# z^T for both row halves by transposes of shifted block pairs, attention matmuls in program order, and the first z turned between score groups

## Chip, cores, metric

The kernel runs on one core of one Trainium2 chip. The metric is the device time of one execution in microseconds (us), the median of several runs. All runs quoted here were fast, that is, none took over 1.5% longer than the fastest run of the same kernel.

## The reference

Shortened:

```python
def _attn_ref(u, v, z):                     # u, v: (8, 3008, 256), z: (8, 3008, 64)
    scores = (1.0 / S) * np.matmul(z, z.transpose(0, 2, 1))
    attn = np.maximum(scores, 0.0) ** 2
    return u * np.matmul(attn, v)
# x is that result as (24064, 256); w_in: (256, 2048), w_out: (2048, 256)
h = x @ w_in
return (h * np.cos(h)) @ w_out
```

The scores are symmetric, so only the 21 block groups on and above the diagonal are computed for each of the 8 batches; the others come from a transpose by DMA (`tt`).

## The kernel before

Four kinds of matmul share TensorE: **S** (scores, contraction over 64 rows), **A** (attention times v), **H** (x times w_in) and **Y** (times w_out). S contracts only 64 rows, so two S matmuls can run at once, one in the upper and one in the lower half of the array. For that, z^T must lie in both halves of the partitions. The kernel before gets it by copying each block of z beside itself on VectorE (DVE) and letting a DMA transpose turn the pair:

```python
    def load_z(b, g):                       # three times per batch, for the batch to come
        n, full, rest = rows(z, b, g)
        j0 = g * G
        nc.gpsimd.dma_start(zst[:, j0:j0 + n, 0, :], full)      # fp32 to fp16, from DRAM
        ...
        nc.vector.tensor_copy(zst[:, j0:j0 + G, 1, :], zst[:, j0:j0 + G, 0, :])
        nc.sync.dma_start_transpose(zT[b % 2][:, j0:j0 + G, :], ...)

    def s_group(b, c, R):
        ...
        t = apool.tile([P, K, K, P], FP16, name="a")            # 8 buffers
        sps = [ps_w.tile([P, CW], FP32, name="w") for k in range(K)]
        for k in reversed(range(K)):
            h = slice((k % 2) * dqk, (k % 2 + 1) * dqk)         # which half of the array
            mm = nc.tensor.matmul(sps[k], zt[h, R * K + k, :], zcols[h, :], start=True, stop=True)
            if k < K - 1:
                tc.keep_in_program_order(mm)
        ...   # ACT: rt = relu(sps); DVE: a = rt * rt
        if R > c:                                               # the mirrored block
            nc.sync.dma_start_transpose(tt..., t...)

    # one chunk of 512 rows: 48 A matmuls into the one acc, then on DVE
    #     x = acc * ut              (ut: u transposed by DMA)
    # H: c16 = cos on ACT, then on DVE g = hp * c16; Y consumes g
```

A scheduler fixes each engine's order when the program is built; on the chip each engine runs its own list in that order. The first z is turned by TensorE in a phase of its own (DVE doubles it, 24 transposes, copies back) before anything else. "Head" below means the first 100 us.

## Time and profile before

| | before |
|---|---|
| median time, us (lowest to highest, 3 runs) | 1407.57 (1403.28 to 1409.5) |
| span of the profiled run, us | 1404.0 |
| TensorE busy | 95% |
| third x starts on DVE (third chunk of attention done), us | 110.2 |
| DVE idle until a z load landed, us | 98.3 |

From the page of the kernel before: the span, TensorE's busy time, the granted TensorE clock in 40 slices of the span (tenths, 9 is 90% or more), and the chain of waits by line. In the profile PE is TensorE, PEld its loading of weights, DVE VectorE, ACT ScalarE, POOL GpSimd and SP SyncE, which issues the DMA transposes; L206 is line 206 of the kernel, x7512 a count, and `out<-in` names what is written and read.

```profile
span 1404.0 us, 19607 instructions
...
PE 1330.1 (95%) x7512; PEld 682.3 (49%) x7512; DVE 782.9 (56%) x1213; ACT 878.8 (63%) x1520; POOL 105.7 (8%) x132
...
PEclk9979999999999999999999999999999999999999
...
PE acc L206 31%; PE w L237 22%; PE yp L256 21%; DMA zst<-in_z_dram 6%; PE w L163 5%; DVE g L244 2%; DMA ut<-ust 2%; ACT rt L170 2%; DMA zT_63<-zst 1%; DVE a L173 1%; SPq L178 1%; DMA zf_82<-in_z_dram 0%; DMA zT_62<-zst 0%; POOL zst L82 0%; POOL ust L103 0%
```

A busy share of 95% looks like a kernel with nothing to win but the last 5%. The chain of waits says otherwise: 6% of the span on it is the load of z, which TensorE does not use for another batch.

Waits of DVE (what it waited for, us in total, times, longest):

```profile
DVE a L173 <- ACT rt L170: 235.3, 289, 7.3
DVE zst L85 <- DMA zst<-in_z_dram: 98.3, 18, 14.2
```

The second line is 98.3 us in 18 waits of DVE for the z load. The copy at L85 itself takes 0.29 us. But DVE runs its list in order, so everything behind the copy waits with it. The Trainium skill ("TensorE: Matmul & The Clock Gate", Part 1, on queue depths) calls the ACT and DVE queues strict FIFO; this trace agrees, for example at 491 us. First DVE, then TensorE, in the timeline (start, duration; in brackets the idle time before and who ended it):

```profile
490.88 0.69 DVE L244 TENSOR_TENSOR g<-w,c_4600 128x512 f16<-128x512 f32 x1 [1.53 <-ACT c_4600 L241]
496.08 0.29 DVE L85 COPY zst<-zst 128x512 f16<-128x512 f16 x1 [4.51 <-DMA zst<-in_z_dram]
496.29 0.68 DVE L244 TENSOR_TENSOR g<-w,c_4611 128x512 f16<-128x512 f32 x1
```

```profile
492.16 0.60 PE L163 MATMUL w<-zT_63 64*128 64x512 f16 x4
492.70 0.61 PE L256 MATMUL yp<-w_out_71,g 128*128 128x256 f16 x4
497.02 1.01 PE L237 MATMUL w<-x,w_in_70 128*128 128x512 f16 x2 [3.72 <-DVE g L244]
497.83 1.06 PE L256 MATMUL yp<-w_out_71,g 128*128 128x256 f16 x4
```

DVE stood 4.5 us until the z load landed; the multiplication that makes g came right behind the copy; TensorE stood 3.7 us for that g. And the matmuls after the stop run at half speed: two H matmuls take 1.01 us where they took 0.59 elsewhere. Waits of TensorE from 100 us on, and three stretches of 175 us (start:end, length, busy time and instructions of PE, PEld, DVE, ACT, POOL, then granted clock, DMA share, GB/s):

```profile
PE w L237 <- DVE g L244: 20.3, 29, 4.0
PE w L163 <- DVE g L244: 13.3, 9, 3.7
```

```profile
350.00:525.00 175.00, 166.12 (x941) 85.16 (x940) 98.78 (x155) 110.45 (x192) 12.34 (x15) 0.98 0.54 89
525.00:700.00 175.00, 164.96 (x952) 86.35 (x950) 99.20 (x155) 111.41 (x193) 13.22 (x16) 0.98 0.63 98
700.00:875.00 175.00, 164.37 (x938) 85.61 (x936) 97.33 (x151) 109.61 (x189) 13.23 (x16) 0.97 0.58 96
```

TensorE waited 33.6 us for g, and the granted clock of 0.98, 0.98 and 0.97 is 3.5 + 3.5 + 5.25 = 12 us of full clock not granted. In the head, the timeline of TensorE has S and A alternating one by one:

```profile
15.89 0.60 PE L163 MATMUL w<-zT_62 64*128 64x512 f16 x1
16.43 0.61 PE L206 MATMUL acc<-a,v_0_64 128*128 128x512 f16 x1
16.98 0.60 PE L163 MATMUL w<-zT_62 64*128 64x512 f16 x1
```

Steps of 0.54 us each, where a warm A matmul takes 0.216. The head is also where the DVE stalls are longest. The ends of the first three chunks on DVE:

```profile
58.37 1.22 DVE L223 TENSOR_TENSOR x<-acc,ut 128x1024 f16<-128x1024 f32 x1
...
88.48 1.22 DVE L223 TENSOR_TENSOR x<-acc,ut 128x1024 f16<-128x1024 f32 x1
...
110.23 1.22 DVE L223 TENSOR_TENSOR x<-acc,ut 128x1024 f16<-128x1024 f32 x1
```

To see how much of the head is lost I priced every matmul with the warm steps of the timeline (0.2165 us for 512 columns, 0.108 for 256, 0.53 for an unbroken group of four S): the whole program is about 1230 us of work by that price, and the first 100 us hold about 36 us of it. This is an estimate worked out from the trace.

### The profile page before, as it was taken

What the parts mean: (1) busy time and instruction counts of PE and PEld (TensorE: products, weight loads), DVE (VectorE), ACT (ScalarE), POOL (GpSimd) and SP (SyncE); (2) the same over time, 40 slices, a digit from 0 to 9 for tenths busy, and PEclk for the clock granted to TensorE, in tenths of its full rate; (3) what the DMA queues carried; (4) which work ended last, traced back from release to release, by engine and by line L of the source; (5) the groups of instructions that cost most, each with busy time, mean ns of one, the idle gap of its engine ahead of it and who ended that gap; (6) DMA issues with size and microseconds to landing.
All of it is one profiled execution on the core that took longest, in us unless ns stands there. A gap on an engine that the chain in (4) does not pass through costs nothing.

```text
span 1404.0 us, 19607 instructions
## 1 busy us (share of the span) xinstructions
PE 1330.1 (95%) x7512; PEld 682.3 (49%) x7512; DVE 782.9 (56%) x1213; ACT 878.8 (63%) x1520; POOL 105.7 (8%) x132
## 2 busy tenths in 40 slices
PE   7769999999999989999898998999999999999998
PEld 1224555445545445454454544555555555555555
DVE  3227564655655555565564655566556556565644
ACT  3337675766666656666565665666666767666645
POOL 3210010000100101000010000100001000000000
PEclk9979999999999999999999999999999999999999
DMA  9994586745836449565494544946559525543201
GB/s 186 179 145 79 88 111 109 124 77 94 119 75 101 84 72 138 86 105 86 75 139 79 103 82 70 146 90 103 91 99 133 98 61 88 102 82 83 61 23 46
DMA packets 447998, 137.13 MB, mean 98 GB/s; under 512 B 397472, under 2 KB 447648, under 8 KB 447904
## 3 DMA queue, kind: packets, MB, share of 16 engines
q1 hardware_dynamic: 323728, 81.53, 32.9%
q0 software_dynamic: 97568, 29.44, 21.3%
q10 hardware_dynamic: 26608, 24.91, 5.9%
q8 instruction: 58, 0.95, 0.3%
q14 instruction: 36, 0.29, 0.1%
HBM read 59.64 MB, written 24.64 MB: 60 GB/s over the span
## 4 chain that ended last, share of the span: by engine, by line
PE 79%; DMA 9%; ACT 4%; DVE 3%; issue 2%; POOL 1%; SPq 1%; POOLq 0%; DVEq 0%; ACTq 0%
PE acc L206 31%; PE w L237 22%; PE yp L256 21%; DMA zst<-in_z_dram 6%; PE w L163 5%; DVE g L244 2%; DMA ut<-ust 2%; ACT rt L170 2%; DMA zT_63<-zst 1%; DVE a L173 1%; SPq L178 1%; DMA zf_82<-in_z_dram 0%; DMA zT_62<-zst 0%; POOL zst L82 0%; POOL ust L103 0%
## 5 line engine op out<-in xcount | busy, mean ns | idle before, releaser
L170 ACT ACTIVATE rt<-w 128x512 f16<-128x512 f32 x672 | 350.6, 601 | 190.2 <-PE w L163 154.8
L237 PE MATMUL w<-x,w_in_70 128*128 128x512 f16 x1504 | 435.8, 382 | 24.7 <-DVE g L244 20.3
L256 PE MATMUL yp<-w_out_71,g 128*128 128x256 f16 x3008 | 450.7, 274 | 1.7 <-ACT ob L264 1.4
L256 PEld LDWEIGHTS <-g 128*128 128x128 f16 x3008 | 287.5, 98 | 220.6 <-issue 62.3
L173 DVE TENSOR_TENSOR a<-rt 128x1024 f16<-128x1024 f16 x336 | 231.1, 691 | 235.3 <-ACT rt L170 235.3
L237 PEld LDWEIGHTS <-w_in_70 128*128 128x128 f16 x1504 | 144.7, 98 | 107.2 <-issue 58.2
L206 PE MATMUL acc<-a,v_2_66 128*128 128x512 f16 x352 | 93.6, 386 | 6.7 <-DVE a L173 6.7
L163 PE MATMUL w<-zT_62 64*128 64x512 f16 x336 | 77.7, 408 | 19.2 <-ACT rt L170 11.1
L264 ACT ACTIVATE ob<-yp 128x512 f32<-128x512 f32 x94 | 56.3, 599 | 58.2 <-PE yp L256 58.2
L206 PE MATMUL acc<-a,v_2_69 128*128 128x512 f16 x352 | 90.4, 379 | 0.0
L103 POOL DMA_DIRECT2D ust<-in_u_dram x48 | 44.4, 928 | 565.7 <-DMA ut<-ust 520.7
L206 PE MATMUL acc<-tt,v_0_64 128*128 128x512 f16 (+1 forms) x288 | 75.0, 387 | 0.0
L206 PE MATMUL acc<-tt,v_0_67 128*128 128x512 f16 (+1 forms) x288 | 71.9, 376 | 0.0
L206 PE MATMUL acc<-a,v_1_65 128*128 128x512 f16 x224 | 65.6, 412 | 4.0 <-DVE x L223 3.9
L223 DVE TENSOR_TENSOR x<-acc,ut 128x128 f16<-128x128 f32 (+7 forms) x89 | 60.3, 715 | 14.0 <-PE acc L206 14.0
L163 PE MATMUL w<-zT_63 64*128 64x512 f16 x336 | 60.8, 382 | 6.2 <-DVE g L244 6.2
L206 PEld LDWEIGHTS <-v_1_65 128*128 128x128 f16 x384 | 37.7, 100 | 59.3 <-issue 24.1
L85 DVE COPY zst<-zst 128x512 f16<-128x512 f16 x21 | 6.2, 294 | 103.5 <-DMA zst<-in_z_dram 98.3
L206 PEld LDWEIGHTS <-v_0_64 128*128 128x128 f16 x384 | 37.9, 100 | 51.8 <-issue 16.2
L206 PEld LDWEIGHTS <-v_2_66 128*128 128x128 f16 x384 | 37.0, 99 | 51.6 <-issue 15.1
L206 PE MATMUL acc<-a,v_1_68 128*128 128x512 f16 x224 | 59.2, 380 | 0.0
L206 PEld LDWEIGHTS <-v_0_67 128*128 128x128 f16 x384 | 37.2, 98 | 42.5 <-issue 4.0
(1547 smaller groups left out, 1368.4 us busy)
## 6 DMA issues: line engine op xcount, KB each, us to landing
out_dram<-ob ACTq DMA_DIRECT2D x94, 256.0 KB, 3.5
ust<-in_u_dram POOLq DMA_DIRECT2D x32, 256.0 KB, 5.9
ust<-in_u_dram POOLq DMA_DIRECT2D x16, 224.0 KB, 6.1
v_0_64<-in_v_dram POOLq DMA_DIRECT2D x4, 512.0 KB, 6.1
v_1_65<-in_v_dram POOLq DMA_DIRECT2D x4, 512.0 KB, 7.1
v_0_67<-in_v_dram POOLq DMA_DIRECT2D x4, 512.0 KB, 6.1
v_1_68<-in_v_dram POOLq DMA_DIRECT2D x4, 512.0 KB, 6.4
tt<-a SPq DMA_TRANSPOSE x120, 5.0
```

Source lines behind the costliest of these rows:

```text
L85: nc.vector.tensor_copy(zst[:, j0:j0 + G, 1, :], zst[:, j0:j0 + G, 0, :])
L103: nc.gpsimd.dma_start(ust[:, dh, 0:n, :], full[:, :, ds])
L163: mm = nc.tensor.matmul(sps[k], zt[h, R * K + k, :], zcols[h, :], start=True, stop=True)
L170: nc.scalar.activation(rt[:, i, :], sps[k0 + i], AF.Relu)
L173: nc.vector.tensor_tensor(tv, rv, rv, ALU.mult)
L178: nc.sync.dma_start_transpose(tt.rearrange("p s k w -> p (s k) w"), t.rearrange("p s k w -> p (s k w)"))
L206: nc.tensor.matmul(acc[:, nh, 0:wn], vt[:, j % G, nh * P:(nh + 1) * P], a, start=(n == 0), stop=(n == NJ - 1))
L223: nc.vector.tensor_tensor(xs[m][:, :, at:at + n], acc[:, :, o:o + n], ut[:, :, i0:i0 + n], ALU.mult)
L237: nc.tensor.matmul(hp, w_in16[:, k, ft * P:(ft + 1) * P], x[:, k, :], start=(k == 0), stop=(k == NDH - 1))
L244: nc.vector.tensor_tensor(gs[(m, ft // FG)][:, ft % FG, :], hp, c16, ALU.mult)
L256: nc.tensor.matmul(ys[m][:, ts % YP, :], gs[(m, ft // FG)][:, ft % FG, ts * P:(ts + 1) * P], w_out16[:, ft, :], start=(n % (YP * NFT) == 0 ...
L264: nc.scalar.activation(ob, ys[m], AF.Copy, bias=0.0, scale=inv_s2)
```

## The change

The intent: no DVE copy. Blocks of z are stored with a zero block at each end, and the transposes take pairs of neighbouring blocks: pair k holds block k-1 and block k, so after the transpose the upper half of the partitions holds one block and the lower half the next, and every block appears in both halves at neighbouring places. Besides, S and A matmuls are tied to program order, the first z is turned between score groups, the first chunk's attention starts earlier, and some preparation moves to other engines.

```diff
-    zst = kpool.tile([P, NJ, 2, dqk], FP16, name="zst")
+    zst = kpool.tile([P, NJ + 2, dqk], FP16, name="zst")
-        nc.vector.tensor_copy(zst[:, j0:j0 + G, 1, :], zst[:, j0:j0 + G, 0, :])
-        nc.sync.dma_start_transpose(
-            zT[b % 2][:, j0:j0 + G, :],
-            zst[:, j0:j0 + G].rearrange("p j h d -> p (j h d)"))
+        for k in range(2):                  # after all three loads of the batch
+            n = (NJ + 2) // 2 - k
+            nc.sync.dma_start_transpose(
+                zT[b % 2][:, k:k + 2 * n - 1:2, :],
+                zst[:, k:k + 2 * n, :].rearrange("p j d -> p (j d)"))
 ... (s_group)
-            mm = nc.tensor.matmul(
-                sps[k], zt[h, R * K + k, :], zcols[h, :], start=True, stop=True)
-            if k < K - 1:
-                tc.keep_in_program_order(mm)
+            lo = k % 2
+            j0 = c * K + 1 - lo
+            chain(nc.tensor.matmul(         # chain: an edge to the S or A matmul before it
+                sps[k], zt[h, R * K + k + 1 - lo, :],
+                zt[h, j0:j0 + K, :].rearrange("p j w -> p (j w)"), start=True, stop=True))
 ... (attention)
-                    nc.tensor.matmul(acc[:, nh, 0:wn], ...)
+                    chain(nc.tensor.matmul(acc[:, nh, 0:wn], ...))
 ... (schedule)
+            early = 10 if b == c == 0 else 0
-                at(b * span + c * U + q, 2, qs[q])
+                at(b * span + c * U + q - early * (1 - q / U), 2, qs[q])
-            for g in range(NG):
-                at(t + (1.0 + 0.75 * g) * U, 0, lambda b=b, g=g: load_z(b, g))
+            at(t + 1.5 * U, 0, lambda b=b: load_z(b))
 ... (cut: the first phase in its own pools goes; first_z_load and first_z_turn become
      scheduled events; ust and v memsets go to POOL; a dummy Relu loads ACT's table early)
```

More of the change, by code (lines that the diff above doesn't have):

```diff
@@ L58 @@
     nc.vector.memset(pihalf, float(math.pi / 2.0))
-    zst = kpool.tile([P, NJ, 2, dqk], FP16, name="zst")
+    zst = kpool.tile([P, NJ + 2, dqk], FP16, name="zst")
     ust = kpool.tile([P, NDH, G, P], FP16, name="ust")
-    zT = [kpool.tile([P, NJ, P], FP16, name=f"zT{i}") for i in range(2)]
+    zT = [kpool.tile([P, NJ + 1, P], FP16, name=f"zT{i}") for i in range(2)]
     vs = [[kpool.tile([P, G, D], FP16, name=f"v{i}_{g}") for g in range(NG)]
           for i in range(2)]
+    ident = kpool.tile([P, P], FP16, name="ident")
     w_in16 = kpool.tile([P, NDH, Dff], FP16, name="w_in16")
     w_out16 = kpool.tile([P, NFT, D], FP16, name="w_out16")
-    for i in range(2):
-        nc.vector.memset(vs[i][NG - 1][:, G - 1, :], 0.0)
     def rows(src, b, g):
@@ L77, in rows, with load_z @@
         return n, full, rest
-    def load_z(b, g):
-        n, full, rest = rows(z, b, g)
-        j0 = g * G
-        nc.gpsimd.dma_start(zst[:, j0:j0 + n, 0, :], full)
-        if rest is not None:
-            nc.gpsimd.dma_start(zst[0:JLAST, j0 + n, 0, :], rest)
-        nc.vector.tensor_copy(zst[:, j0:j0 + G, 1, :], zst[:, j0:j0 + G, 0, :])
-        nc.sync.dma_start_transpose(
-            zT[b % 2][:, j0:j0 + G, :],
-            zst[:, j0:j0 + G].rearrange("p j h d -> p (j h d)"))
+    def load_z(b):
+        for g in range(NG):
+            n, full, rest = rows(z, b, g)
+            j0 = g * G + 1
+            nc.gpsimd.dma_start(zst[:, j0:j0 + n, :], full)
+            if rest is not None:
+                nc.gpsimd.dma_start(zst[0:JLAST, j0 + n, :], rest)
+        for k in range(2):
[3 more added lines that the diff above has]
+                zst[:, k:k + 2 * n, :].rearrange("p j d -> p (j d)"))
     def load_v(b, g):
@@ L110, in load_u @@
         uts[(b, g)] = ut
-    with tc.tile_pool(name="first", bufs=1) as fpool, \
-            tc.tile_pool(name="ps_first", bufs=NG, space=bass.MemoryType.PSUM) as fps:
-        zf = [fpool.tile([P, G, dqk], FP32, name=f"zf{g}") for g in range(NG)]
-        ident = fpool.tile([P, P], FP16, name="ident")
-        make_identity(nc, ident)
-        nc.vector.memset(zf[NG - 1][:, G - 1, :], 0.0)
-        for g in range(NG):
-            n, full, rest = rows(z, 0, g)
-            eng = (nc.sync, nc.scalar, nc.sync)[g % 3]
-            eng.dma_start(zf[g][:, 0:n, :], full)
-            if rest is not None:
-                eng.dma_start(zf[g][0:JLAST, n, :], rest)
-        for g in range(NG):
-            load_v(0, g)
-        for g in range(NG):
-            j0 = g * G
-            for h in range(2):
-                nc.vector.tensor_copy(zst[:, j0:j0 + G, h, :], zf[g])
-            tp = fps.tile([P, G, P], FP16, name="tp")
-            for j in range(G):
-                nc.tensor.transpose(
-                    tp[:, j, :], zst[:, j0 + j].rearrange("p h d -> p (h d)"), ident)
-            nc.vector.tensor_copy(zT[0][:, j0:j0 + G, :], tp)
-        nc.vector.memset(zst[:, NJ - 1, 0, :], 0.0)
     psum = lambda name, bufs: ctx.enter_context(
@@ L150, with first_z_load, first_z_turn, chain @@
     ps_y = psum("ps_y", 1)
+    zfs = {}
+    def first_z_load(g):
+        zfs[g] = xpool.tile([P, NDH, TW], FP16, name="x")
+        zf = zfs[g].rearrange("p h w -> p (h w)").bitcast(FP32).rearrange(
+            "p (j d) -> p j d", d=dqk)
+        zfs[g] = zf
+        n, full, rest = rows(z, 0, g)
+        eng = (nc.sync, nc.scalar, nc.sync)[g % 3]
+        if rest is not None:
+            nc.vector.memset(zf[:, n, :], 0.0)
+        eng.dma_start(zf[:, 0:n, :], full)
+        if rest is not None:
+            eng.dma_start(zf[0:JLAST, n, :], rest)
+    def first_z_turn(g):
+        j0 = g * G
+        last = g == NG - 1
+        nc.vector.tensor_copy(zst[:, j0 + 1:j0 + 1 + G, :], zfs[g])
+        for k, n in ((0, G), (G, 1))[0:1 + last]:
+            tp = ps_w.tile([P, CW], FP32, name="w").bitcast(FP16).rearrange(
+                "p (j w) -> p j w", w=P)
+            for i in range(n):
+                nc.tensor.transpose(
+                    tp[:, i, :],
+                    zst[:, j0 + k + i:j0 + k + i + 2, :].rearrange("p j d -> p (j d)"),
+                    ident)
+            nc.vector.tensor_copy(zT[0][:, j0 + k:j0 + k + n, :], tp[:, 0:n, :])
     fresh = {}
     turned = {}
+    before = []
+    def chain(mm):
+        if before:
+            tc.add_manual_dep(
+                mm.ins, before.pop().name,
+                mybir.DependencyInfo(
+                    mybir.DependencyClass.NoSync, mybir.DependencyReason.DATA),
+                reason="order")
+        before.append(mm.ins)
     def s_group(b, c, R):
         zt = zT[b % 2]
-        zcols = zt.rearrange("p j w -> p (j w)")[:, c * CW:(c + 1) * CW]
         t = apool.tile([P, K, K, P], FP16, name="a")
@@ L161, in s_group @@
         for k in reversed(range(K)):
-            h = slice((k % 2) * dqk, (k % 2 + 1) * dqk)
-            mm = nc.tensor.matmul(
-                sps[k], zt[h, R * K + k, :], zcols[h, :], start=True, stop=True)
-            if k < K - 1:
-                tc.keep_in_program_order(mm)
+            lo = k % 2
+            h = slice(lo * dqk, (lo + 1) * dqk)
+            j0 = c * K + 1 - lo
+            chain(nc.tensor.matmul(
+                sps[k], zt[h, R * K + k + 1 - lo, :],
+                zt[h, j0:j0 + K, :].rearrange("p j w -> p (j w)"),
+                start=True, stop=True))
         for k0 in range(0, K, 2):
@@ L205, in quantum @@
                 for nh in range(NDH):
-                    nc.tensor.matmul(
+                    chain(nc.tensor.matmul(
                         acc[:, nh, 0:wn], vt[:, j % G, nh * P:(nh + 1) * P], a,
-                        start=(n == 0), stop=(n == NJ - 1))
+                        start=(n == 0), stop=(n == NJ - 1)))
             if (q + 1) * per >= NJ:
@@ L295 @@
         if b == 0:
-            base = -100.0
-            at(base, 0, lambda: load_u(0, 0))
-            at(base + 1, 0, lambda: nc.gpsimd.dma_start(
+            for g in range(NG):
+                at(-100 + g, 0, lambda g=g: first_z_load(g))
+                at(-30 + 4.5 * g if g == 0 else -14.5 + 4.57 * (g - 0.5), 0,
+                   lambda g=g: first_z_turn(g))
+                at(-80 + g, 0, lambda g=g: load_v(0, g))
+            at(-70, 0, lambda: load_u(0, 0))
+            at(-69, 0, lambda: nc.gpsimd.dma_start(
                 w_in16, moe_w_in.rearrange("(k p) f -> p k f", p=P)))
-            at(base + 2, 0, lambda: nc.gpsimd.dma_start(
+            at(-68, 0, lambda: nc.gpsimd.dma_start(
                 w_out16, moe_w_out.rearrange("(k p) f -> p k f", p=P)))
-            at(base + 3, 0, lambda: load_u(0, 1))
+            at(-67, 0, lambda: load_u(0, 1))
         else:
             t = (b - 1) * span
-            for g in range(NG):
-                at(t + (1.0 + 0.75 * g) * U, 0, lambda b=b, g=g: load_z(b, g))
+            at(t + 1.5 * U, 0, lambda b=b: load_z(b))
             for g in range(NG):
@@ L313, with prepare @@
         at(t + 3.0 * U, 0, lambda b=b: load_u(b, 2))
-    nc.vector.memset(ust, 0.0)
+    dummy = kpool.tile([P, 1], FP32, name="dummy")
+    def prepare():
+        nc.scalar.activation(dummy, pihalf, AF.Relu)
+        make_identity(nc, ident)
+        nc.vector.memset(zst[:, 0, :], 0.0)
+        nc.vector.memset(zst[:, NJ + 1, :], 0.0)
+        nc.gpsimd.memset(ust, 0.0)
+        for i in range(2):
+            nc.gpsimd.memset(vs[i][NG - 1][:, G - 1, :], 0.0)
+    at(-90, 0, prepare)
     events.sort(key=lambda e: e[:3])
```

## The prediction

> **What bounds the kernel now.** TensorE: the page shows PE busy 95% of 1404 us; in the stage table 1050 to 1225 us is busy 173.8 of 175. In the timeline a warm 512-column matmul starts every 0.2165 us, a 256-column one every 0.108, and an unbroken score group (four K=64 matmuls, two in each half of the array) takes 0.53. At these prices the 7512 matmuls are about 1235 us of work (estimate). Laid on the timeline, the first 100 us hold only 36 us of work, 100 to 850 loses about 80 us, and 850 to the end 1.65 us per 50.
>
> **What the change removes.**
> 1. The 21 DVE copies of z (294 ns each) are cheap, but DVE runs in order: the waits view charges 98 us of DVE idle to them, for the z load (5.8 us to landing). The chain of waits gives these loads 5.6%. 35 us lie in the head (two of 14.2 and 13.3). From 122 to 848 us there are 14 stalls of 2 to 7 us; PE idles behind the late g for about 30 us there, and the granted clock falls to 0.97 in places, which I price at 8 to 10 us. The shifted transposes move 25 blocks per batch instead of 24: no new cost.
> 2. Order. From 15 to 49 us score and attention matmuls alternate one by one, 0.54 us each. The Trainium skill, "TensorEngine Tiling (Array Packing)", Key Properties, says that changing the tiling mode drains the engine; the trace agrees (warm, alternating ones step 0.31 us, not 0.2165). The new head is S4 A6 S4 A6. But h and y matmuls can still split score groups: single score matmuls fall only from 84 runs to 56, the gain nearly all in the head. A split group costs about 1.1 us more, so 15 to 20 us of splits stay.
> 3. Start: first score at about 7 us instead of 11.5, the ACT table load (1.28 us) hidden, c=0 attention earlier.
>
> **What it adds.** Memsets on POOL ahead of the v loads, delaying v, u and weights by an estimated 3 us.
>
> **The head after.** ACT paces it: 4 activations in 2.06 us per group against 0.53+1.30 us of PE. The first x still needs the u transpose, which landed at 30.7 us (now about 33), and the third chunk needs a turned block queued on SP behind the second u transpose (issued at 41.65) and two transposes of about 5 us: about 60 us. I put the third x at 65 us instead of 110.2: 45 us won.
>
> **Sum.** 45 (head) + 38 (stalls and cold clock after 100 us) = 83: span about 1321, measured about 1325 us, 80% range 1306 to 1346. Faster by over 2%: 0.96; same 0.035; slower 0.005.
>
> **What would show each step.** No DVE waits on z loads; PE waits on g in 400 to 850 us falling from about 27 us to under 6; PEclk 1.0 in all slices after the first three; third x at 60 to 70 us; first 100 us holding about 75 us of work; score matmul busy time falling by 15 to 25 us of 138; split groups between 100 and 550 us still there; last 550 us unchanged.
>
> **What would make it wrong.** Head: the DMA queues (mean share over 1.0 in the first 80 us) may hold turned blocks or u back longer, so that it wins only 30; or PE stays at the slow clock while ACT paces it, since the skill ("TensorE: Matmul & The Clock Gate", Part 1) makes the clock follow recent activity, and before stayed slow to about 50 us. Middle: SP waits for all of z and delays turned blocks. Or split groups vanish: down to 1305.

## The result

| | before | after |
|---|---|---|
| median time, us (lowest to highest, 4 runs) | 1407.67 (1403.28 to 1409.5) | 1333.43 (1332.07 to 1333.52) |
| span of the profiled run, us | 1404.0 | 1331.7 |
| third x starts on DVE, us | 110.2 | 81.1 |
| priced work in the first 100 us (estimate as above) | about 36 | about 62 |
| S matmul busy time, us | 138.5 | 122.1 |

The ratio after to before is 0.9475 (95% interval 0.9452 to 0.9497), so 5% faster. Ratios here are the mean time of one kernel's fast runs over that of the other's of the same rounds, so not quite the ratio of the medians.

The page of the changed kernel, the same parts:

```profile
span 1331.7 us, 19537 instructions
...
PE 1293.3 (97%) x7513; PEld 675.3 (51%) x7513; DVE 777.1 (58%) x1188; ACT 876.8 (66%) x1521; POOL 107.9 (8%) x135
...
PEclk9899999999999999999999999999999999999999
...
PE acc L224 36%; PE w L255 25%; PE yp L274 24%; PE w L181 6%; ACT rt L188 2%; DVE g L262 2%; DMA tt<-a 1%; DMA ut<-ust 1%; DMA x<-in_z_dram 0%; DVE a L191 0%; DVE x L241 0%; ACT ob L282 0%; ACT L259 0%; DVE zT_62 L155 0%; SPq L139 0%
```

The z load of the later batches is gone from the chain; the one left is the first batch's. DVE's waits:

```profile
DVE a L191 <- ACT rt L188: 255.0, 310, 4.4
...
DVE a L191 <- DMA tt<-a: 10.2, 1, 10.2
DVE x L241 <- DMA ut<-ust: 5.2, 1, 5.2
DVE zst L146 <- DMA x<-in_z_dram: 4.4, 2, 3.8
```

What is left on DVE for z (L146) is the first batch's cast. Two new entries, 10.2 and 5.2 us, are waits for DMA transposes, and both lie in the head. TensorE's waits for g from 100 us on and the three stretches:

```profile
PE w L255 <- DVE g L262: 4.8, 22, 0.3
```

```profile
350.00:525.00 175.00, 173.51 (x1012) 90.75 (x1011) 103.74 (x159) 117.60 (x205) 13.26 (x16) 1.00 0.62 101
525.00:700.00 175.00, 173.61 (x1026) 91.88 (x1025) 106.80 (x164) 118.61 (x206) 13.26 (x16) 1.00 0.64 105
700.00:875.00 175.00, 173.80 (x1028) 92.16 (x1025) 105.45 (x162) 120.47 (x209) 13.25 (x16) 1.00 0.60 100
```

The wait for g fell from 33.6 to 4.8 us and the clock is 1.00. In the head, TensorE and DVE:

```profile
11.07 2.09 PE L224 MATMUL acc<-a,v_0_64 128*128 128x512 f16 x6
...
13.63 1.47 PE L224 MATMUL acc<-a,v_0_64 128*128 128x512 f16 x6
...
35.78 2.72 PE L224 MATMUL acc<-a,v_0_64 128*128 128x512 f16 x6 [6.33 <-DVE x L241]
...
64.67 1.01 PE L224 MATMUL acc<-a,v_2_66 128*128 128x512 f16 x2 [5.84 <-DVE a L191]
```

```profile
34.51 1.23 DVE L241 TENSOR_TENSOR x<-acc,ut 128x1024 f16<-128x1024 f32 x1 [5.24 <-DMA ut<-ust]
...
63.93 1.29 DVE L191 TENSOR_TENSOR a<-rt 128x1024 f16<-128x1024 f16 x2 [10.23 <-DMA tt<-a]
...
81.06 1.21 DVE L241 TENSOR_TENSOR x<-acc,ut 128x1024 f16<-128x1024 f32 x1
```

A comes in runs of six and S in groups of four now, warm (six A in 1.47 us) from 13.6 us on. But then TensorE stands: at 35.8 us behind the first x, and at 64.7 us behind an `a` tile. After each stop the clock is slow again (six A in 2.72 us), as the Trainium skill ("TensorE: Matmul & The Clock Gate", Part 1) has it for a TensorE that has stood idle for some microseconds. The chain of waits shows what both waited for:

```profile
22.67 11.74 DMA ut<-ust
...
51.25 12.55 DMA tt<-a
```

A transpose of u took 11.7 us and one of a score tile 12.6 us from issue to release. Over this whole run a u transpose lands in a median of 4.8 us and a score tile's in 4.7.

Of the 72.3 us of span, 29.2 were won by the end of the third chunk (110.2 to 81.1) and 43.1 after it (1293.8 to 1250.6 us from there to the end).

### The profile page after: what moved, and what is told of

Read it like the earlier page. It is cut to its first block, busy times and chain, and to the rows that moved or that the text cites. A ratio compares the mean times of both kernels' runs of the same rounds, so it can differ in the third digit from the quotient of the medians.

```text
span 1331.7 us, 19537 instructions
## 1 busy us (share of the span) xinstructions
PE 1293.3 (97%) x7513; PEld 675.3 (51%) x7513; DVE 777.1 (58%) x1188; ACT 876.8 (66%) x1521; POOL 107.9 (8%) x135
## 4 chain that ended last, share of the span: by engine, by line
PE 90%; ACT 4%; DVE 2%; DMA 2%; issue 1%; SPq 0%; DVEq 0%; ACTq 0%
PE acc L224 36%; PE w L255 25%; PE yp L274 24%; PE w L181 6%; ACT rt L188 2%; DVE g L262 2%; DMA tt<-a 1%; DMA ut<-ust 1%; DMA x<-in_z_dram 0%; DVE a L191 0%; DVE x L241 0%; ACT ob L282 0%; ACT L259 0%; DVE zT_62 L155 0%; SPq L139 0%
## 5 line engine op out<-in xcount | busy, mean ns | idle before, releaser
L255 PEld LDWEIGHTS <-w_in_71 128*128 128x128 f16 x1504 | 143.7, 98 | 87.6 <-issue 42.4
L224 PE MATMUL acc<-a,v_2_66 128*128 128x512 f16 x352 | 91.8, 387 | 5.8 <-DVE a L191 5.8
L224 PE MATMUL acc<-a,v_2_69 128*128 128x512 f16 x352 | 89.7, 379 | 0.0
L224 PE MATMUL acc<-tt,v_0_64 128*128 128x512 f16 (+1 forms) x288 | 71.7, 373 | 0.0
L241 DVE TENSOR_TENSOR x<-acc,ut 128x128 f16<-128x128 f32 (+7 forms) x89 | 60.3, 715 | 18.9 <-PE acc L224 13.6
L224 PE MATMUL acc<-tt,v_0_67 128*128 128x512 f16 (+1 forms) x288 | 71.2, 373 | 0.0
L181 PE MATMUL w<-zT_62 64*128 64x512 f16 x336 | 63.0, 392 | 2.5 <-DVE zT_62 L155 1.9
L224 PEld LDWEIGHTS <-v_0_64 128*128 128x128 f16 x384 | 37.1, 99 | 53.6 <-issue 15.2
L224 PEld LDWEIGHTS <-v_2_66 128*128 128x128 f16 x384 | 37.2, 99 | 52.9 <-issue 13.9
L224 PE MATMUL acc<-a,v_1_65 128*128 128x512 f16 x224 | 58.7, 387 | 3.6 <-DVE x L241 3.6
L224 PEld LDWEIGHTS <-v_1_65 128*128 128x128 f16 x384 | 37.3, 99 | 48.0 <-issue 9.5
L181 PE MATMUL w<-zT_63 64*128 64x512 f16 x336 | 59.1, 381 | 0.0
L224 PEld LDWEIGHTS <-v_2_69 128*128 128x128 f16 x384 | 37.1, 98 | 42.8 <-issue 2.4
L224 PEld LDWEIGHTS <-v_1_68 128*128 128x128 f16 x384 | 37.0, 98 | 42.4 <-issue 3.3
L224 PEld LDWEIGHTS <-v_0_67 128*128 128x128 f16 x384 | 37.0, 98 | 42.0 <-issue 2.7
```

Of the source, the lines that this page charges most:

```text
L181: chain(nc.tensor.matmul(sps[k], zt[h, R * K + k + 1 - lo, :], zt[h, j0:j0 + K, :].rearrange("p j w -> p (j w)"), start=True, stop=True))
L224: chain(nc.tensor.matmul(acc[:, nh, 0:wn], vt[:, j % G, nh * P:(nh + 1) * P], a, start=(n == 0), stop=(n == NJ - 1)))
L241: nc.vector.tensor_tensor(xs[m][:, :, at:at + n], acc[:, :, o:o + n], ut[:, :, i0:i0 + n], ALU.mult)
L255: nc.tensor.matmul(hp, w_in16[:, k, ft * P:(ft + 1) * P], x[:, k, :], start=(k == 0), stop=(k == NDH - 1))
```

## The experiments

Three parts of the change could be worth the time: **Z** (no copy, shifted pairs), **C** (program order of S and A) and **H** (the new head). My theory was that Z gives the middle, and that the order and the start give much of the head. I ran each part alone and each left out, then Z's mechanism by itself, then what is left in the head.

| run | what it is | median us | ratio to before of the same rounds, 95% | third x, us |
|---|---|---|---|---|
| before | | 1407.7 | 1 | 110.2 |
| after | Z, C, H | 1333.4 | 0.9475 (0.9452 to 0.9497) | 81.1 |
| m_late | before, copies placed later | 1336.9 | 0.9495 (0.9478 to 0.9512) | 84.6 |
| f_z | Z alone | 1336.5 | 0.9493 (0.9477 to 0.9509) | 83.4 |
| f_c | C alone | 1408.6 | 1.0004 (0.9980 to 1.0029) | 112.7 |
| f_h | H alone | 1405.6 | 0.9983 (0.9955 to 1.0012) | 109.9 |
| f_zc | Z and C | 1334.3 | 0.9490 (0.9474 to 0.9507) | 82.5 |
| f_zh | Z and H | 1335.3 | 0.9498 (0.9481 to 0.9516) | 81.4 |
| f_ch | C and H | 1402.5 | 0.9982 (0.9964 to 1.0001) | 109.8 |
| h_wv | after, weight and v loads later | 1337.4 | 0.9492 (0.9467 to 0.9518) | 85.6 |
| h_v | after, v loads later | 1333.5 | 0.9483 (0.9467 to 0.9499) | 80.7 |
| h_a9 | after, nine `a` buffers | 1329.7 | 0.9453 (0.9440 to 0.9466) | 77.5 |
| h_va | after, both | 1327.6 | 0.9438 (0.9426 to 0.9451) | 74.4 |
| h_now | after, weights not loaded | 1329.4 | 0.9448 (0.9435 to 0.9460) | 76.6 |

All gave the right result except h_now.

### m_late: the copies stay, the wait goes

```diff
-        nc.vector.tensor_copy(zst[:, j0:j0 + G, 1, :], zst[:, j0:j0 + G, 0, :])
-        nc.sync.dma_start_transpose(...)
+    def turn_z(b, g):
+        copy = nc.vector.tensor_copy(zst[:, j0:j0 + G, 1, :], zst[:, j0:j0 + G, 0, :])
+        <an ordering edge on DVE: copy behind the latest x multiplication>
+        nc.sync.dma_start_transpose(...)
 ...
-                at(t + (1.0 + 0.75 * g) * U, 0, lambda: load_z(b, g))
+                at(t + (0.5 + 0.25 * g) * U, 0, lambda: load_z(b, g))
+                at(t + (3.0 + 0.75 * g) * U, 5, lambda: turn_z(b, g))
```

> The kernel before, PE order unchanged, all 21 DVE copies and 21 transposes of z kept, but each copy is placed on DVE behind a later x multiplication, about 25 us after its load. Theory (the copies cost only because DVE, in order, stood waiting for the load): DVE waits on z loads fall from 98 us to under 5, and time falls to 1345 to 1365 us, with PE waits on g after 100 us under 8 us. Rival (the copies' own time, 6 us in all, or the number of transposes and SP issues, is what costs): 1395 us or more.

Measured: 1336.9 us. All 21 copies are there and take 0.283 us each, none waits for a load, and TensorE has the same list of matmuls in the same order as before, but for one A matmul that moved by two places. Its wait for g from 100 us on:

```profile
PE w L247 <- DVE g L254: 4.8, 22, 0.3
```

That is the changed kernel's number to the tenth. So the copies themselves cost next to nothing; the wait that they brought into DVE's queue cost about 71 us (1407.5 in the same rounds, less 1336.9). The loads of z also come a little earlier in the program here, and the transposes follow the later copies; f_z below leaves the loads about where they were and comes out the same. The theory named the cause, and undersized it: I had expected to be left at 1345 or above, because I credited part of the head to other causes.

### f_z, f_c, f_h: each part alone

f_z has the first phase of before with the new z layout; f_c replaces `keep_in_program_order` by `chain` for S and A; f_h is the changed kernel with the z layout and copy of before and without `chain`.

> Before with the z part of the change alone (shifted pairs, two transposes per batch, no copy; first phase and PE order as before). Theory: about the same as m_late, 1345 to 1365 us, since both take away the same wait; 100 us onward as good as in the whole change, head still with one-by-one score and attention matmuls. Rival (order of matmuls and head carry the gain): above 1385.

> Before with the program order of attention matmuls alone. Theory: single score runs gone from the head only, while the DVE still waits for z loads there; 1390 to 1404 us, score matmul busy time down by about 15 us of 138. Rival (splits of score groups are the main loss): below 1375.

> Before with the new head alone (first z turned between score groups, early c=0 attention, memsets on POOL, table load hidden), copies and PE ordering rule as before. Theory: the head's start is earlier but the DVE stalls on z loads at 30 to 87 us come at the same DMA times: 1385 to 1402 us. Rival (the head rearrangement carries the head's 29 us by itself): 1370 to 1380.

Measured: 1336.5, 1408.6 and 1405.6 us. All three lie outside the ranges that I expected: f_z came out below its range, the two others above theirs. I had given Z too little and the other parts too much. Z alone is as good as m_late, whose transposes differ in number and shape, so those play no part that can be seen. C alone and H alone give nothing: both intervals include 1. f_c did lower the busy time of S from 138.5 to 132.9 us (about 15 us less was expected), and f_h to 127.9, and no time came of it, because DVE still stood for 112.3 and 107.5 us until z loads landed.

What is more, f_z still alternates S and A one by one at half speed in the head, and yet its third chunk ends at 83.4 us, where the changed kernel's ends at 81.1. From f_z's timeline of TensorE:

```profile
41.09 0.61 PE L168 MATMUL w<-zT 64*128 64x512 f16 x1
...
45.18 0.60 PE L168 MATMUL w<-zT 64*128 64x512 f16 x1
45.72 3.43 PE L213 MATMUL acc<-a,v 128*128 128x512 f16 x10
49.09 0.61 PE L168 MATMUL w<-zT 64*128 64x512 f16 x4
```

TensorE is recorded busy without a gap until 45 us, slowly, doing what the changed kernel does fast, only to wait afterwards. (The granted clock of the profile reads 1.00 in this stretch, although A matmuls that follow each other start 0.40 to 0.43 us apart; the steps of the matmuls tell more here than that record.) As I read the two timelines, the rearranged head's gain went into the waits for DMA transposes; no run tests that by itself.

### f_zc, f_zh, f_ch: each part left out

> The whole change without the new head (first phase in its own pool as before). With z alone at 1336.5 and all three at 1333.4, order and head are worth 3 us together. If what paces the head is data (transposes of u and of squared scores by DMA), order alone adds little: 1334 to 1337 us. If the order is the part that pays: 1333.

> The whole change without the program order of attention matmuls. Data-paced head: 1333 to 1336 us. If order pays: 1336 or more.

> The whole change without its z part: DVE copies back, order and new head kept. If the wait for the z load in DVE's queue is the whole gain: 1398 to 1408 us, equal to before, although single score runs are gone from the head. If order and head pay when they are together: below 1390.

Measured: 1334.3, 1335.3 and 1402.5 us. Without Z, the two other parts together gain nothing that is clear of noise (0.9982, 0.9964 to 1.0001). DVE waits of f_ch:

```profile
DVE zst L84 <- DMA zst<-in_z_dram: 108.5, 19, 22.7
```

With Z, the four kernels f_z, f_zc, f_zh and after lie within 3.1 us of each other and their intervals overlap: C and H together are worth about 3 us in the medians, and how the 3 us split is not resolved.

### h_wv, h_v, h_a9, h_va: what holds the head now

These change the changed kernel's order of loads on POOL, or one buffer count. In all of them TensorE's order is the changed kernel's; in all but h_wv, SP's is too.

```diff
 h_wv: w_in and w_out loads behind the second u load; next batch's v loads behind the third u load
 h_v:  only the v loads
-    apool = pool("a", 8)
+    apool = pool("a", 9)          # h_a9; h_va is h_v and this
```

> The changed kernel with the issue order on POOL alone altered: the two weight loads (2 MB) go behind the second u load, and the next batch's v loads (1.5 MB) behind the third u load of the batch before. Theory (the head waits for two DMA transposes, u's of 11.7 us and a turned block's of 12.6 us, which are slow because bulk loads share the 16 DMA engines): u's transpose lands in 5 to 8 us, first x at 26 to 30 us instead of 34.5, third x at 66 to 74 instead of 81.1, time 1319 to 1327 us. Rival (transposes are slow by themselves in the head, or ACT and the clock pace it): 1331 to 1335.

> The changed kernel with only the next batch's v loads (1.5 MB) held behind the third u load; weights where they were; the same order on TensorE and SP. If bulk loads make the turned block that PE waited for at 64.7 us late: first x still at 34 to 35 us, that block lands in 5 to 8 us instead of 12.6, third x at 72 to 77 us instead of 81.1, time 1325 to 1330 us. If the wait only moves to the next transposes, as in h_wv: third x above 79, 1331 to 1336.

> The changed kernel with nine a buffers instead of eight. DVE's 10 us wait at 53 to 64 us was for a transpose of an a tile to finish before the tile could be written again. If the number of buffers holds the head: third x 4 us or more earlier, 1327 to 1330 us. If DMA throughput holds it (transposes come late anyway and attention waits for them): within 2 us of 1333.4.

> Both: v loads held back and nine a buffers. If both waits are real and separate: 1322 to 1328 us. If DMA bytes set the head whatever the order: 1330 to 1335.

h_wv: 1337.4 us, a miss. Its five runs spread from 1330.9 to 1339.0 (the profiled one took 1338.1), and its interval overlaps that of after, so it is not shown to be slower than after. The first x came at 29.4 us, as expected, but the third at 85.6. The chain in its head:

```profile
33.32 23.83 DMA tt<-a
...
67.57 16.08 DMA tt<-a
```

The 11.7 us wait for u was replaced by one of 23.8 us for a turned score tile: the weight loads, issued between 29.2 and 31.0 us now, had been moved on top of it. The Trainium skill ("DMA: Bandwidth & Descriptors", Issuing engines are not separate DMA queues) says that DMAs of all issuing engines run on the same 16 DMA engines and interleave. That fits this run: loads issued from POOL made a transpose issued from SP late. But the run changed more than was meant: on POOL the next batch's z loads moved up too, from 36.7 to 9.4 us.

h_v: 1333.5 us with a third chunk at 80.7, so the rival holds: alone, it only moves the wait. It is the cleaner test of what makes a transpose slow, since SP's order stayed the same. The transpose that took 12.6 us in after (the seventh on SP) lands in 4.4 us here, and a turned score tile issued at 53.6 us, with the third u load and then the v loads issued from 52.1 us on, takes 15.7. Counted by queue in the traces, from 50 to 55 us SP's transposes moved 60 GB/s in after, beside 122 GB/s of POOL's loads, and 203 GB/s in h_v, where POOL's loads moved nothing.

h_a9: 1329.7 us, third chunk 3.6 us earlier (4 or more were expected): with eight buffers DVE had to wait for a transpose to finish reading a tile before writing it again. The ninth buffer doesn't remove that wait: DVE still stands 9.6 us for the same transpose, one tile later. In h_va, with the v loads held back too, no wait of DVE for a score tile's transpose is left in the head.

h_va: 1327.6 us, third chunk at 74.4, 5.9 us below h_v of the same rounds with intervals that do not overlap. It is the fastest correct kernel here. Its chain in the head still holds two slow transposes:

```profile
22.42 11.79 DMA ut<-ust
...
53.94 14.55 DMA tt<-a
```

### h_now: fewer bytes in the head

```diff
-            at(-69, 0, lambda: nc.gpsimd.dma_start(w_in16, ...))
-            at(-68, 0, lambda: nc.gpsimd.dma_start(w_out16, ...))
+            at(-69, 0, lambda: nc.gpsimd.memset(w_in16, 0.01))
+            at(-68, 0, lambda: nc.gpsimd.memset(w_out16, 0.01))
```

> Wrong result on purpose: the changed kernel with both weight loads (2 MB in fp16) replaced by memsets of a constant on POOL, which is idle there; the same order on TensorE and SP. This takes bytes off the DMA engines in the head and nothing else. If DMA throughput paces the head: 2 MB at the measured 178 GB/s are 11 us, so first x near 28 us, third x at 68 to 73, time 1321 to 1326 us. If order, clock or ACT pace it: above 1330.

Measured: 1329.4 us, third chunk at 76.6, but the first x at 38.4 instead of the 28 that I expected. The run is spoiled by my substitute. DVE, then POOL:

```profile
4.78 11.50 DVE L146 CAST zst<-x 128x512 f16<-128x512 f32 x3 [3.73 <-DMA x<-in_z_dram]
```

```profile
8.63 3.58 POOL L321 MEMSET w_in<- 128x4096 f16 x1
12.08 3.58 POOL L322 MEMSET w_out<- 128x4096 f16 x1
```

Of the three casts of the first z, one took 10.41 us instead of 0.41: it began at 5.54 us and ended only after POOL's second memset had ended. The Trainium skill ("SBUF — State Buffer", Terms, shared port pair) says that DVE and GpSimd share a pair of SBUF ports under an exclusive lock, and that the loser fully blocks. This trace fits that, but the cast is recorded as starting 3.1 us before the first memset, so which of the two held the ports first is not shown. The late start was made up and the kernel still came out 4 us ahead of after in the medians (the intervals overlap), and the u transpose landed in 5.1 us instead of 11.7. That leans towards the bytes, but with two things changed it settles no size.

## Why the prediction was right or wrong

The time was predicted as 1325 us (1306 to 1346) and came out at 1333.4. The direction and the main cause were right. Of the 83 us in its sum, 72 were won: one term was 16 us too large and the other 5 us too small, so some of the nearness is luck, and two of the three causes listed for the head gave nothing by themselves.

- **DVE stalls after 100 us, 38 us predicted: right, 43 measured.** The wait of TensorE for g fell by 28.8 us (33.6 to 4.8), and 12 us of clock came back; m_late and f_z show that the wait alone does it (1336.9 and 1336.5).
- **Head, 45 us predicted: 29 measured.** The step that failed is "I put the third x at 65 us instead of 110.2". It came at 81.1. I had listed the u transpose at 33 us correctly (34.5), but charged the turned blocks "about 5 us" each; the one that TensorE waited for took 12.6 us, with plain loads on the same DMA engines (4.4 us in h_v, where the v loads came later), and DVE waited for it because it needed the tile's `a` buffer again, which I had not counted. A ninth buffer moved the third chunk by 3.6 us and buffers and v loads together by 6.7 (81.1 to 74.4). My estimate of 75 us of work in the first 100 us was 62 for the same reason.
- **What the head owes its gain to: partly wrong.** Point 1 did place 35 us of DVE stalls in the head, but I listed order (point 2) and start (point 3) beside it as gains of the head and did not split the 45 us. Alone they give 1.0004 and 0.9983, together without Z 0.9982. Z alone brings the third chunk to 83.4 us, which is 26.9 of the 29.2 us. The longest DVE stalls of all (14.2 and 13.3 us) lay in the head; the alternating matmuls were slow, but making them faster won nothing while these stalls and the DMA transposes set the pace.
- **The last 550 us: unchanged, as predicted.** From the same x multiplication to the end, the two kernels take 535.6 and 535.5 us; no z loads remain there in the kernel before.
- **Split score groups: as predicted, and harmless to the sum.** S busy time fell by 16.4 us (15 to 25 predicted). In the instruction order, single S runs fell from 84 to 56. Tying H and Y to the order as well was not run, so what it would give is not shown.
- **POOL memsets delaying v, u and weights by 3 us: right in kind.** The first v load was issued at 3.47 us instead of 1.27.
- **The dangers I named.** That the DMA queues "may hold turned blocks or u back longer, so that it wins only 30" is what happened. TensorE staying slow did happen, but only after each stop.

What stays open is how much of the remaining loss in the head (about 31 us of the first 100 even in h_va, by the same pricing) is bytes on the DMA engines, and how much is the order in which SP issues transposes: h_now was meant to tell and did not cleanly. That bulk loads make single transposes slow is shown (12.6 against 4.4 us in h_v); what that is worth in time is not, since h_v alone gained nothing.

## What to carry to other kernels

Look in the chain of waits for loads that nothing needs yet: an instruction of 0.3 us that waits for a load on an in-order engine holds everything behind it, and placing it later in the queue is worth as much as removing it (1336.9 against 1336.5 us). A faster order on a busy engine gains nothing while its inputs come later than that engine's slow order would use them; test each part of a change alone before crediting it. When moving a bulk load away from one late transfer, check which transfer it lands on: h_wv cured an 11.7 us wait and made one of 23.8.

## What the Trainium skill lacked or had wrong

- "TensorE: Matmul & The Clock Gate", Part 1 puts the full clock after about 3.4 us of sustained activity. In f_z TensorE is recorded busy without a gap from 12.9 to 45.7 us, alternating S and A one by one, and stays at half rate (A matmuls that follow each other start 0.40 to 0.43 us apart); it sped up about 2.3 us after A matmuls came in a run at 45.7 us (0.217 us apart from 48.1). Why it stayed slow, for instance because an S matmul fills only half of the rows, no run tests.
- "TensorEngine Tiling (Array Packing)", Key Properties says that a change of tiling mode drains the engine, without a price. Here a warm step across the change is 0.31 us against 0.216 within a run: about 0.095 us per change.
- "DMA: Bandwidth & Descriptors" gives a bandwidth for DMA transposes, but no page found here says what one costs beside plain loads: a score tile's transpose has a median of 4.7 us to landing over the run of after, and 12.6 us (after) and 23.8 us (h_wv) on the chain in the head; the transpose of 12.6 us took 4.4 in h_v, with hardly a load beside it.
